# Third unit's state in 64x64 tiles, gate sums of two chunks turned on VectorE, x of two more units through DRAM

## The chip, the core and the metric

The kernel runs on one core of a Trainium2 chip. The engines are TensorE (PE; PEld is its weight load), VectorE (DVE), ScalarE (ACT), GpSimd (POOL) and SyncE (SP), which here issues nearly all DMAs. The metric is the time of one execution in microseconds (us). Three runs of the kernel before took 430.86 to 431.17 us, median 430.98 us.

## What is computed

An mLSTM over 768 time steps for 4 batches of 8 heads of size 40, and a gated two-layer network on its output. In the reference, cut to what matters:

```python
for t in range(S):                                   # B, H, S, D = 4, 8, 768, 40
    m_new  = maximum(f_gate[t] + m, i_gate[t])
    f_stab = exp(f_gate[t] + m - m_new); i_stab = exp(i_gate[t] - m_new); m = m_new
    C = f_stab * C + i_stab * outer(v[t], k[t])      # 40x40 state per head
    n = f_stab * n + i_stab * k[t]
    y[t] = sigmoid(o_gate[t]) * (C @ q[t]) / maximum(abs(n @ q[t]), 1)
x = y as (3072, 320)
h = x @ w_in                                         # 320 -> 2048
out = (h * sigmoid(h)) @ w_out                       # 2048 -> 320
```

## The kernel before

**Units.** Time is cut into 12 chunks of 64. A unit is one chunk of two of the four batches: 24 units, counted from 0; "the third unit" is unit 2. A unit holds 128 rows of tokens (two batches of 64 steps). It makes scores from q and k, weighs them with a decay matrix `D`, adds the contribution of the state `Cm`, normalizes, and gates with o. The result is `x`, 128 tokens by 320 features. It also adds `k` weighted by `kw` times `v` to the state: the matmuls are in `state` (line 692), their sum lies in the tile `pu`, and `carry` (line 735) adds it to `Cm` on VectorE.

**Steps.** Three units make a step of the network: 384 tokens, 8 steps (0 to 7). A step goes through 16 blocks of 128 hidden features, called blocks 0 to 15 here (`fc` in the code). For each, `mm1` multiplies x with w_in into the PSUM tile `ph`, `act` makes tanh on ScalarE (`th`) and the product on VectorE (`g`), and `mm2`, two blocks later, multiplies with w_out into `pout`. So the last two `mm2` of a step come after the first two `mm1` of the next. In step 0 the weights are taken in 32-bit form; from step 1 on every operand is split into a rounded part and a remainder (x into `xh` and `xl`, w_in into `wh` and `wl`), and products of the parts are summed.

**Order.** The order of every engine's instructions is written by hand; no scheduler moves them, and each engine runs its own queue in order. While step j is multiplied, the three units of step j+1 are worked in between, at the blocks that `PLACES` (line 41) gives: in step 0, unit 3 at block 5, unit 4 at block 9, unit 5 at block 12. The table `FILL` (line 1076) adds, for step 0 alone, what is left of the start: making weight parts (`wmake`, which also issues the load of the next part, line 261), the gate sums of later chunks, loads. DMAs issued by SyncE also stand in one queue in order; one that waits holds those behind it.

**x.** mm1 needs x with the features on the partitions. There are two ways. `xpose` (line 784) lets TensorE transpose it by three matmuls against a unit matrix into PSUM, and `xput` (line 796) splits it: xh by ScalarE (line 805), xl by VectorE (line 806). Or, for units in the set `AROUND` (line 930), `turn_out` (line 761) transposes 32x32 blocks on VectorE (line 766) and writes them to DRAM by four DMAs (line 768), `turn_in` (line 772) reads them back two blocks after the unit's place into `px` in SBUF (line 776), and `xput` follows six blocks after the place. Before, units 6 to 23 but unit 8 go around.

**Gate sums.** Running sums of the gates, per batch and head, are made with heads on the partitions (`i_t`) and needed with time on the partitions (`aT`). For chunks 2 and 3 `spread` (line 188) transposes them with TensorE and copies them by VectorE (line 207); for chunks 4 to 11 `spread_far` (line 216) does it with two VectorE transposes (line 228) and four ScalarE copies (line 233).

Of the kernel before, what the change touches and what calls it, by code (L numbers as in the profile page):

```python
# [8 lines left out]
F32 = mybir.dt.float32  # L9
# [5 lines left out]
ALU = mybir.AluOpType  # L15
# [3 lines left out]
B, H, S, D = 4, 8, 768, 40  # L19
L = 64  # L20
NC = S // L
NP = B // 2
NU = NC * NP
# [3 lines left out]
UPS = 3  # L27
# [16 lines left out]
def mlstm_mlp_kernel(  # L44
# [12 lines left out]
    nc = tc.nc  # L57
# [6 lines left out]
    psO = pool("psO", 3, space=PSUM)  # L64
    psH = pool("psH", 2, space=PSUM)
    psP = pool("psP", 1, space=PSUM)
    psU = pool("psU", 1, space=PSUM)
# [9 lines left out]
    ident = cp.tile([128, 128], F32, name="ident")  # L77
# [3 lines left out]
    for k in range(2):  # L81
        m = mask[k * L : (k + 1) * L]
        nc.gpsimd.affine_select(
            out=m, in_=m, compare_op=ALU.is_ge, fill=NEG, base=0,
# [18 lines left out]
    BH = B * H  # L103
    f_t, i_t, m_t, LF, pat = (home[:BH, k * S : (k + 1) * S] for k in range(5))
    aT = cp.tile([128, NC, NP, H], F32, name="aT")

    LFd = dr.tile([NC, BH, L], F32, name="LFd")
# [78 lines left out]
        yield  # L186

    def spread(lo, hi, eng):

        c0, c1 = lo // L, hi // L  # L190
        eng.dma_start(
            LFd[c0:c1].rearrange("c r t -> r c t"),
            LF[:, lo:hi].rearrange("r (c t) -> r c t", t=L),
        )
        yield
        pt = psU.tile([128, 512], F32, tag="u", name=f"pt{lo}")

        for c in range(c0 - 1, c1):
            w = slice(c * L, (c + 2 - (c == NC - 1)) * L)
            nc.tensor.transpose(  # L200
                pt[: w.stop - w.start, c * BH : (c + 1) * BH], i_t[:, w], ident[:BH, :BH]
            )
            if (c - c0) % 3 == 1:
                yield
        for k in range(2):
            r = slice(k * L, (k + 1) * L)
            nc.vector.tensor_copy(  # L207
                aT[r, c0:c1, :, :],
                pt[r, (c0 - k) * BH : (c1 - k) * BH].rearrange(
                    "p (c q d h) -> p c q d h", q=NP, d=2, h=H  # L210
                )[:, :, :, k, :],
            )
        yield


    def spread_far(lo, hi, eng):

        c0, c1 = lo // L, hi // L
        eng.dma_start(
            LFd[c0:c1].rearrange("c r t -> r c t"),  # L220
            LF[:, lo:hi].rearrange("r (c t) -> r c t", t=L),
        )
        yield
        n = (c1 - c0) * BH
        src = i_t[:, lo:hi].rearrange("r (c b x) -> r b c x", b=2, x=32)
        at = home[:BH, : 2 * n].rearrange("x (b c r) -> x b c r", b=2, r=BH)
        for b in range(2):
            nc.vector.transpose(at[:, b], src[:, b])
            yield
        for k in range(2):  # L230
            for b in range(2):
                r = k * L + b * 32
                nc.scalar.copy(
                    aT[r : r + 32, c0:c1].rearrange("p c q h -> p (c q) h"),
                    at[:, b].rearrange("x c (q d h) -> x (c q) d h", q=NP, d=2)[:, :, k, :],
                )
            yield
# [114 lines left out]
    def wload(n):  # L352
        for p in parts[nload[0] : nload[0] + n]:
            p.load()
        nload[0] = min(nload[0] + n, len(parts))

    def wmake(n):

        for p in parts[nmade[0] : nmade[0] + n]:
            p.make()  # L360
            wload(1)
        nmade[0] = min(nmade[0] + n, len(parts))
# [10 lines left out]
    def bank(n, pool_, tag, shape, name):  # L373

        if n < UPS:
            return pool_.tile(shape, F32, tag=tag, name=name)
        return psU.tile(shape, F32, tag="u", name=name)
# [5 lines left out]
    class Unit:  # L383
# [308 lines left out]
        def state(self):  # L692
            n, c, p = self.n, self.c, self.p
            if c == NC - 1:
                return
            if n >= UPS:
                self.pu = [
                    pool_.tile([128, 4, D1], F32, tag=tag, name=f"pu{n}_{tag}")
                    for pool_, tag in ((psU, "u"), (psH, "h"))
                ]  # L700
                for j in range(4):
                    for d in range(2):
                        r = slice(d * L, (d + 1) * L)
                        for a in range(2):
                            nc.tensor.matmul(  # L705
                                self.pu[d][a * 64 : a * 64 + D, j, :],
                                self.kw[r, a * 4 + j, :],
                                self.vt[r, d, a * 4 + j, :],
                                start=True,
                                stop=True,  # L710
                            )
                return
            pu = bank(n, psO, "o", [128, H, D1], f"pu{n}")
            by_d = pu.rearrange("p (d j) f -> p j d f", d=2)
            for j in range(4):
                for a in range(2):
                    nc.tensor.matmul(  # L717
                        by_d[a * 64 : a * 64 + D, j],
                        self.kw[:, a * 4 + j, :],
                        self.vt[:, :, a * 4 + j, :],  # L720
                        start=True,
                        stop=True,
                    )
            self.pu = pu
# [10 lines left out]
        def carry(self, copy=nc.scalar.copy, steps=(0, 1)):  # L735
            n, c, p = self.n, self.c, self.p
            if c == NC - 1:
                return
            pu = self.pu
            for a in range(2):  # L740
                r = slice(a * 64, a * 64 + D)
                v = Cm[p][r, a, :].rearrange("p (h e) -> p h e", e=D1)
                if c == 0:
                    copy(v, pu[r])
                    continue
                if 0 in steps:
                    nc.gpsimd.tensor_tensor(  # L747
                        out=v,
                        in0=v,
                        in1=self.lq[r, :, L - 1].unsqueeze(2).broadcast_to([D, H, D1]),  # L750
                        op=ALU.mult,
                    )
                if 1 not in steps:
                    continue
                for d in range(2) if n >= UPS else ():
                    w = v[:, d * 4 : (d + 1) * 4]
                    nc.vector.tensor_tensor(out=w, in0=w, in1=pu[d][r], op=ALU.add)
                if n < UPS:
                    nc.vector.tensor_tensor(out=v, in0=v, in1=pu[r], op=ALU.add)

        def turn_out(self):

# [164 lines left out]


    units = [Unit(n) for n in range(NU)]
    AROUND = set(range(2 * UPS, NU)) - {3 * UPS - 1}  # L930
    steps = {}

    def block(n):
# [18 lines left out]
    def turn(n):  # L952
# [5 lines left out]
        if n % UPS == 0:  # L958
            steps[n // UPS] = Step(n // UPS)
        if n not in AROUND:  # L960
            units[n].xpose()
            units[n].xput(steps[n // UPS])

    def run(n, it):
        for _ in range(n):
            next(it, None)

    u0, u1, u2, u3, u4 = units[:5]
# [29 lines left out]
    for _ in range(2):  # L998
        nc.tensor.matmul(  # L999
            dummy, ident, ident.unsqueeze(1).broadcast_to([128, 4, 128]), start=True, stop=True  # L1000
        )
    two = gates(2 * L, 4 * L)
    near, far = spread(2 * L, 4 * L, nc.gpsimd), spread_far(4 * L, S, nc.gpsimd)
    late = [gates(4 * L, 8 * L), gates(8 * L, S)]
    widen()
    run(5, gates(0, 2 * L))
# [76 lines left out]
            run(1, near),  # L1083
            u3.reach_act(),
        ),
        1: lambda: (wmake(1), u3.expo_act(), u3.keep(), u3.near(), u4.load_qk()),
        2: lambda: (
            u3.scores(),
            u3.weigh(),
# [45 lines left out]
    for j in range(NSTEP):  # L1135
        st = steps[j]
        for fc in range(NFC):
# [6 lines left out]
            if 0 in at:  # L1144
# [4 lines left out]
                at[0].carry(steps=(0, 1) if j == 0 else (0,))  # L1149
                if at[0].n in AROUND:  # L1150
                    at[0].turn_out()
# [18 lines left out]
            if 1 in at:  # L1170
                turn(at[1].n)
                if j == 0:
                    units[at[1].n + 2].add()
            if 6 in at and at[6].n in AROUND:
                at[6].xput(steps[j + 1])
            if 2 in at and at[2].n in AROUND:
                at[2].turn_in()
# [80 lines left out]
```

## Time and profile before

| what | value |
| --- | --- |
| three runs, median | 430.98 us |
| the profiled execution | 431.02 us |
| its span, first to last instruction | 429.2 us |
| TensorE busy | 422.4 us, 98% |
| VectorE busy | 288.5 us, 67% |
| ScalarE busy | 220.6 us, 51% |
| GpSimd busy | 124.8 us, 29% |

The profile is of one execution, on the only core. A timeline row gives an instruction's start from the span's beginning, its length, engine, line, operation, what it writes and reads, and in brackets the idle time of the engine before it with the instruction that ended it, where that is long enough to be shown. Merged rows (x3) give the length of all together. A 32-bit matmul shows as two records. Matmuls overlap, so what one costs TensorE is the distance to the next one's start.

### The profile page before, as it was taken

The numbers are of one execution on the slowest core, as the hardware profiler recorded it, in microseconds if no ns is written. First come the engines' busy times: TensorE is split into PE (matmuls) and PEld (weight loads), VectorE is DVE, ScalarE is ACT, GpSimd is POOL, SyncE is SP. The second block draws the span as 40 slices with busy tenths as digits, with TensorE's granted clock in tenths as the row PEclk, the third lists the DMA queues.
The fourth block names the chain that finished last, engine by engine and source line by source line (L and its number), as shares of the span: only waits on it lengthen the run. The fifth ranks groups of instructions, "written<-read, shape, count | busy, mean of one in ns | idle before, by whom it ended". The sixth has DMA issues, their size and how long they took to land.

```text
span 429.2 us, 12518 instructions
## 1 busy us (share of the span) xinstructions
PE 422.4 (98%) x5062; PEld 391.7 (91%) x5062; DVE 288.5 (67%) x650; ACT 220.6 (51%) x481; POOL 124.8 (29%) x135
## 2 busy tenths in 40 slices
PE   8999999999999999999999999999999999999995
PEld 4767677899999999999999999999999999999995
DVE  5888799877887677467765677566764756443342
ACT  7684866755755454454454644444454543353331
POOL 5734135234234423043412344034320400000000
PEclk9999999999999999999999999999999999999999
DMA  8999696334551775127660575316750231001001
GB/s 272 387 366 311 177 299 165 117 89 141 159 169 21 196 196 155 31 61 189 174 172 2 123 218 139 118 25 179 209 163 22 54 94 20 18 9 39 2 2 46
DMA packets 62650, 57.17 MB, mean 133 GB/s; under 512 B 31440, under 2 KB 49184, under 8 KB 62592
## 3 DMA queue, kind: packets, MB, share of 16 engines
q1 hardware_dynamic: 62288, 55.94, 45.7%
q8 instruction: 40, 0.66, 0.7%
q10 hardware_dynamic: 208, 0.26, 0.2%
q0 software_dynamic: 96, 0.16, 0.1%
q14 instruction: 18, 0.15, 0.1%
HBM read 48.99 MB, written 7.36 MB: 131 GB/s over the span
## 4 chain that ended last, share of the span: by engine, by line
PE 80%; issue 17%; DVE 1%; ACT 1%; POOL 0%; POOLq 0%; ACTq 0%; DVEq 0%
PE ph L849 35%; PE pout L901 33%; PE p L549 3%; PE p L637 2%; PE p L620 2%; PE dummy L999 1%; PE pu_u L705 1%; PE pu_h L705 1%; DVE D L576 0%; PE e L396 0%; PE px L794 0%; PE pu L717 0%; PE po L604 0%; PE p L794 0%; POOL qt L533 0%
## 5 line engine op out<-in xcount | busy, mean ns | idle before, releaser
L856 ACT ACTIVATE th<-ph 128x384 f32<-128x384 f32 x128 | 62.4, 488 | 106.7 <-PE ph L849 106.2
L849 PE MATMUL ph<-xh,wh 128*128 128x384 f32 x336 | 113.8, 339 | 0.0
L849 PE MATMUL ph<-xl,wh 128*128 128x384 f32 x336 | 113.6, 338 | 0.0
L901 PE MATMUL pout<-woh,gh 128*128 128x320 f32 x336 | 105.5, 314 | 0.0
L901 PE MATMUL pout<-woh,gl 128*128 128x320 f32 x336 | 103.9, 309 | 0.0
L901 PE MATMUL pout<-wol,gh 128*128 128x320 f32 x336 | 103.3, 307 | 0.0
L876 ACT CAST gh<-th 128x384 fp32r<-128x384 f32 x112 | 57.5, 513 | 81.3 <-DVE th L871 69.9
L880 DVE TENSOR_TENSOR gl<-th,gh 128x384 fp32r<-128x384 f32 x112 | 64.6, 577 | 47.5 <-ACT gh L876 47.5
L871 DVE SCALAR_TENSOR_TENSOR th<-th,ph 128x384 f32<-128x384 f32 x112 | 61.4, 548 | 51.1 <-ACT th L856 50.6
L849 PE MATMUL ph<-xh,wl 128*128 128x384 f32 x224 | 75.9, 339 | 0.0
L747 POOL TENSOR_TENSOR Cm<-Cm,lq 40x328 f32<-40x328 f32 x40 | 30.6, 764 | 114.6 <-PE p L637 111.8
L901 PEld LDWEIGHTS pout<-woh,gh 128*128 128x128 f32 x336 | 63.0, 188 | 0.9
L849 PEld LDWEIGHTS ph<-xh,wh 128*128 128x128 f32 x336 | 63.1, 188 | 0.2
L849 PEld LDWEIGHTS ph<-xl,wh 128*128 128x128 f32 x336 | 63.0, 188 | 0.2
L901 PEld LDWEIGHTS pout<-woh,gl 128*128 128x128 f32 x336 | 63.0, 188 | 0.1
L901 PEld LDWEIGHTS pout<-wol,gh 128*128 128x128 f32 x336 | 63.1, 188 | 0.0
L533 POOL TENSOR_TENSOR qt<-qk,lq 104x512 f32<-104x512 f32 x22 | 29.7, 1348 | 99.4 <-ACT lq L529 89.3
L849 PEld LDWEIGHTS ph<-xh,wl 128*128 128x128 f32 x224 | 42.1, 188 | 0.0
L901 PE MATMUL pout<-wo,g 128*128 128x320 f32 x96 | 28.7, 435 | 0.0
L516 POOL TENSOR_TENSOR D<-D,am 128x512 f32<-128x512 f32 x20 | 26.1, 1303 | 4.0 <-DMA D<-LFd 2.5
L508 POOL TENSOR_TENSOR am<-mask,aT 128x512 f32<-128x512 f32 x20 | 24.1, 1205 | 6.6 <-DVE aT L207 5.1
L576 DVE TENSOR_TENSOR D<-p,D 128x512 f32<-128x512 f32 x24 | 16.5, 689 | 13.7 <-PE p L637 12.3
(136 smaller groups left out, 524.4 us busy)
## 6 DMA issues: line engine op xcount, KB each, us to landing
qk<-in_qk_dram SPq DMA_DIRECT2D x24, 512.0 KB, 5.1
ko<-in_ko_dram SPq DMA_DIRECT2D x24, 320.0 KB, 5.3
wro<-in_w_out_dram SPq DMA_DIRECT2D x8, 640.0 KB, 7.3
D<-LFd SPq DMA_DIRECT2D x40, 128.0 KB, 3.1
lq<-LFd SPq DMA_DIRECT2D x40, 128.0 KB, 4.9
wri<-in_w_in_dram SPq DMA_DIRECT2D x8, 512.0 KB, 6.0
vb<-in_vp_dram SPq DMA_DIRECT2D x48, 82.0 KB, 5.1
out_dram<-ob SPq DMA_DIRECT2D x45, 80.0 KB, 2.1
```

Of the source, the lines that this page charges most:

```text
L508: nc.gpsimd.tensor_tensor(out=self.am, in0=mask.unsqueeze(1).broadcast_to([128, H, L]), in1=aT[:, self.c, self.p, :].unsqueeze(2).broadcas ...
L516: nc.gpsimd.tensor_tensor(out=self.Dm, in0=self.Dm, in1=self.am, op=ALU.add)
L533: nc.gpsimd.tensor_tensor(out=self.qt, in0=self.q[:KS], in1=self.lq[:KS], op=ALU.mult)
L549: nc.tensor.matmul(self.ps[d * L : (d + 1) * L, a * 4 + j, :], self.k[r, d * 4 + j, :], self.q[r, d * 4 + j, :], start=True, stop=True,)
L576: nc.vector.tensor_tensor(out=self.Dm, in0=self.ps, in1=self.Dm, op=ALU.mult)
L747: nc.gpsimd.tensor_tensor(out=v, in0=v, in1=self.lq[r, :, L - 1].unsqueeze(2).broadcast_to([D, H, D1]), op=ALU.mult,)
L849: nc.tensor.matmul(ph, w, x, start=(i == 0), stop=(i == len(ops) - 1))
L856: nc.scalar.activation(th, ph, AF.Tanh, scale=0.5)
L871: nc.vector.scalar_tensor_tensor(out=th, in0=th, scalar=1.0, in1=ph, op0=ALU.add, op1=ALU.mult)
L876: nc.scalar.copy(gh, th)
L880: nc.vector.tensor_tensor(out=gl, in0=th, in1=gh.bitcast(F32), op=ALU.subtract)
L901: nc.tensor.matmul(self.po[t], g[:, ts], w, start=(fc == 0 and i == 0), stop=(last and i == len(ops) - 1),)
```

## The change

Three edits, all within step 0 and the start before it.

1. Unit 2's state is multiplied in 64x64 tiles, as the units from 3 on do it: the two halves of the rows apart, into two PSUM tiles (`pu_u` and, for unit 2, `pu_o`), 16 matmuls of 41 columns in place of 8 of 82 columns. `carry` adds the halves with four VectorE instructions in place of two.
2. `spread` becomes what `spread_far` was, for chunks 2 and 3 too: two VectorE transposes and four ScalarE copies in place of three TensorE transposes and two VectorE copies. The VectorE transposes stand in `FILL[1]`, the copies in `FILL[2]`.
3. Units 3 and 4 go around through DRAM like the later ones (unit 5, like unit 8, stays with TensorE). Their `xput` moves from the block after their place to the end of block 11 and of block 15.

```diff
     def spread(lo, hi, eng):
...
-        pt = psU.tile([128, 512], F32, tag="u", name=f"pt{lo}")
-        for c in range(c0 - 1, c1):
...
-            nc.tensor.transpose(
-                pt[: w.stop - w.start, c * BH : (c + 1) * BH], i_t[:, w], ident[:BH, :BH]
-            )
...
-    def spread_far(lo, hi, eng):
...
         for b in range(2):
             nc.vector.transpose(at[:, b], src[:, b])
             yield
...
@@ def state
-            if n >= UPS:
+            if n > 1:
                 self.pu = [
                     pool_.tile([128, 4, D1], F32, tag=tag, name=f"pu{n}_{tag}")
-                    for pool_, tag in ((psU, "u"), (psH, "h"))
+                    for pool_, tag in ((psU, "u"), (psH, "h") if n >= UPS else (psO, "o"))
                 ]
@@ def carry
-                for d in range(2) if n >= UPS else ():
+                for d in range(2) if n > 1 else ():
                     w = v[:, d * 4 : (d + 1) * 4]
                     nc.vector.tensor_tensor(out=w, in0=w, in1=pu[d][r], op=ALU.add)
-                if n < UPS:
-                    nc.vector.tensor_tensor(out=v, in0=v, in1=pu[r], op=ALU.add)
...
-    AROUND = set(range(2 * UPS, NU)) - {3 * UPS - 1}
+    AROUND = set(range(UPS, NU)) - {2 * UPS - 1, 3 * UPS - 1}
...
-    near, far = spread(2 * L, 4 * L, nc.gpsimd), spread_far(4 * L, S, nc.gpsimd)
+    near, far = (spread(lo, hi, nc.gpsimd) for lo, hi in ((2 * L, 4 * L), (4 * L, S)))
...
-        1: lambda: (wmake(1), u3.expo_act(), u3.keep(), u3.near(), u4.load_qk()),
+        1: lambda: (run(2, near), wmake(1), u3.expo_act(), u3.keep(), u3.near(), u4.load_qk()),
```

VectorE at the end of step 0, before. `kw7` is unit 7's key weights, `g0_15` the product of block 15, `wl2` the remainder of the third w_in part; `th1_0` is the first product of step 1.

```order
L863 SCALAR_TENSOR_TENSOR g0_14_1233<-th0_14_1229,ph0_14_1224 128x384
L327 TENSOR_TENSOR wl1_1231<-wi1_514,wh_103 128x512
L228 STREAM_TRANSPOSE home_107<-home_107 32x256
L568 TENSOR_TENSOR kw7_1254<-ko7_1092,D7_1085 128x320
L863 SCALAR_TENSOR_TENSOR g0_15_1265<-th0_15_1261,ph0_15_1256 128x384
L327 TENSOR_TENSOR wl2_1263<-wi2_570,wh_103 128x512
L871 SCALAR_TENSOR_TENSOR th1_0_1284<-th1_0_1284,ph1_0_1275 128x384
```

The same place of VectorE now; `xl1` is the xl tile of step 1, `px4` unit 4's x as read back.

```order
L833 SCALAR_TENSOR_TENSOR g0_14_1252<-th0_14_1248,ph0_14_1243 128x384
L299 TENSOR_TENSOR wl1_1250<-wi1_514,wh_103 128x512
L200 STREAM_TRANSPOSE home_107<-home_107 32x256
L540 TENSOR_TENSOR kw7_1273<-ko7_1111,D7_1104 128x320
L833 SCALAR_TENSOR_TENSOR g0_15_1284<-th0_15_1280,ph0_15_1275 128x384
L299 TENSOR_TENSOR wl2_1282<-wi2_583,wh_103 128x512
L776 TENSOR_TENSOR xl1_845<-px4_1088,xh1_844 128x3x128
L841 SCALAR_TENSOR_TENSOR th1_0_1305<-th1_0_1305,ph1_0_1296 128x384
```

Unit 4's xl has moved from behind block 10 to this place, the last of step 0; the rest stands as it did.

SyncE's DMA queue from the loads of unit 5 (`D5`, `qk5`, `vb2`, `ko5`) on, before; `wro4` is the load of the fifth w_out part, `wrc6` and `wri6` parts of w_in, `lq5` the decay of unit 5.

```order
L464 DMA qk5_706<-in_qk_dram 128x1024
L484 DMA vb2_142<-in_vp_dram 64x328 x2
L475 DMA ko5_710<-in_ko_dram 128x640
L261 DMA wro4_808<-in_w_out_dram 128x2x640
L496 DMA lq5_822<-LFd_115 64x2x256 x2
L261 DMA wrc6_843<-in_w_tail_dram 128x512
L261 DMA wri6_849<-in_w_in_dram 128x2x512
L261 DMA wro5_874<-in_w_out_dram 128x2x640
```

The same place now; `xd1` is the DRAM buffer, `xt3` unit 3's transposed blocks, `px3` its x read back.

```order
L436 DMA qk5_717<-in_qk_dram 128x1024
L456 DMA vb2_142<-in_vp_dram 64x328 x2
L447 DMA ko5_721<-in_ko_dram 128x640
L738 DMA xd1_117<-xt3_812 32x12x32 x4
L233 DMA wro4_825<-in_w_out_dram 128x2x640
L468 DMA lq5_839<-LFd_115 64x2x256 x2
L233 DMA wrc6_855<-in_w_tail_dram 128x512
L233 DMA wri6_861<-in_w_in_dram 128x2x512
L746 DMA px3_882<-xd1_117 128x3x128
L233 DMA wro5_888<-in_w_out_dram 128x2x640
```

The four writes of unit 3's x stand ahead of five loads that stood directly behind `ko5`, and the read stands between two weight loads. Unit 4's five DMAs stand in the same way ahead of the last two w_out parts and of unit 7's loads.

## Rows read from the trace of the kernel before

**Rows 1.** Page, part 1: busy time, share of the span and instructions by engine

```profile
PE 422.4 (98%) x5062; PEld 391.7 (91%) x5062; DVE 288.5 (67%) x650; ACT 220.6 (51%) x481; POOL 124.8 (29%) x135
```

**Rows 2.** Stretches: length; busy PE, PEld, DVE, ACT, POOL; PEclk; DMA share, GB/s

```profile
65.80:80.30 14.50, 14.47 (x138) 10.76 (x131) 14.20 (x30) 9.58 (x21) 7.03 (x7) 1.00 0.63 183
...
78.60:381.70 303.10, 302.83 (x3861) 296.19 (x3860) 206.34 (x466) 148.08 (x329) 86.75 (x82) 1.00 0.42 112
```

**Rows 3.** Timeline of PE: start, length, line, operation; state and transposes

```profile
21.77 0.77 PE L717 MATMUL pu<-vb,kw 128*40 128x82 f32 x16
22.47 1.56 PE L849 MATMUL ph<-x,wi 128*128 128x384 f32 x4
...
28.18 0.37 PE L200 MATMUL pt<-ident,home 32*128 32x32 f32 x3
...
43.67 0.49 PE L794 MATMUL p<-ident,x 128*128 128x128 f32 x3
43.99 1.46 PE L849 MATMUL ph<-x,wi 128*128 128x384 f32 x4
...
66.35 0.21 PE L705 MATMUL pu_u<-vb,kw 64*40 64x41 f32 x2
...
66.67 0.44 PE L637 MATMUL p<-Cm,qt 40*64 40x41 f32 x16
```

**Rows 4.** Line 766 by itself: count, length in ns (min/median/max), first, last start

```profile
L766 DVE STREAM_TRANSPOSE xt<-x x17: 578/578/580, 91.5 to 360.1; 128x384 f32<-128x384 f32 x17
```

**Rows 5.** Timeline of PE where step 1 begins

```profile
78.61 0.58 PE L849 MATMUL ph<-xh,wh 128*128 128x384 f32 x1
79.03 0.34 PE L849 MATMUL ph<-xl,wh 128*128 128x384 f32 x1
```

**Rows 6.** Timeline of DVE in step 0; in brackets idle time before

```profile
42.20 1.05 DVE L757 TENSOR_TENSOR Cm<-Cm,pk 40x164 f32<-40x164 f32 x1
...
53.83 0.81 DVE L282 SCALAR_TENSOR_TENSOR wo<-wro 128x640 uint32<-128x640 uint32 x1
...
65.78 0.81 DVE L282 SCALAR_TENSOR_TENSOR wi<-wri 128x512 uint32<-128x512 uint32 x1 [0.43 <-ACT wri L281]
...
70.68 0.97 DVE L757 TENSOR_TENSOR Cm<-Cm,pk 40x164 f32<-40x164 f32 x1
...
79.65 0.67 DVE L327 TENSOR_TENSOR wl<-wi,wh 128x512 fp32r<-128x512 f32 x1
```

**Rows 7.** Line 806 by itself: the instruction that writes xl

```profile
L806 DVE TENSOR_TENSOR xl<-px,xh x17: 548/1358/1367, 110.6 to 376.6; 128x384 fp32r<-128x384 f32 x17
L806 DVE TENSOR_TENSOR xl<-p,xh x4: 551/554/558, 44.7 to 126.3; 128x384 fp32r<-128x384 f32 x4
```

**Rows 8.** Timeline of POOL around the end of step 0

```profile
64.68 1.36 POOL L533 TENSOR_TENSOR qt<-qk,lq 104x512 f32<-104x512 f32 x1 [5.54 <-ACT lq L529]
...
76.74 2.17 POOL L533 TENSOR_TENSOR qt<-qk,lq 104x512 f32<-104x512 f32 x1 [4.71 <-ACT lq L529]
88.38 1.56 POOL L747 TENSOR_TENSOR Cm<-Cm,lq 40x328 f32<-40x328 f32 x2 [9.47 <-PE p L637]
```

**Rows 9.** Lines 757 and 568 by themselves: Cm adds and kw

```profile
L757 DVE TENSOR_TENSOR Cm<-Cm,pk x38: 312/322/1046, 41.6 to 338.4; 40x164 f32<-40x164 f32 x38
...
L568 DVE TENSOR_TENSOR kw<-ko,D x18: 454/492/1315, 36.8 to 307.3; 128x320 f32<-128x320 f32 x18
```

**Rows 10.** Timeline of the DMA issues on SP

```profile
36.83 0.39 SPq L261 DMA_DIRECT2D wro<-in_w_out_dram  x1
...
92.12 1.88 SPq L768 DMA_DIRECT2D xd<-xt  x4
```

**Rows 11.** Line 261 by itself: from issue to landing of the weight loads

```profile
DMA to landing us min/median/max: 3.3/6.0/8.2
```

**Rows 12.** Timeline of ACT: fifth w_out part, tanh of block 15

```profile
51.17 0.79 ACT L280 ACTIVATE wro<-wro 128x640 f32<-128x640 f32 x1
...
77.44 0.49 ACT L856 ACTIVATE th<-ph 128x384 f32<-128x384 f32 x1 [0.77 <-PE ph L849]
```

More of the change, by code (lines that the diff above doesn't have):

```diff
@@ L188, in spread @@
     def spread(lo, hi, eng):
[L190 to L193, printed above, removed]
-        )
-        yield
-        pt = psU.tile([128, 512], F32, tag="u", name=f"pt{lo}")
-        for c in range(c0 - 1, c1):
-            w = slice(c * L, (c + 2 - (c == NC - 1)) * L)
-            nc.tensor.transpose(
-                pt[: w.stop - w.start, c * BH : (c + 1) * BH], i_t[:, w], ident[:BH, :BH]
[L202 to L213, printed above, removed]
-    def spread_far(lo, hi, eng):
         c0, c1 = lo // L, hi // L
```

## The prediction

> **What bounds the kernel now.** I read the busy shares of the page first. TensorE is busy 98% of the span, no other engine over 67% [rows 1]: what counts is TensorE's own work, and any moment in which it must wait. Then the table by stretches: from 78.6 to 381.7 us TensorE is busy 302.83 of 303.10 us, at the full clock, 2.4 GHz [rows 2]. So a delay that exists at 78.6 us, where step 0 hands over to step 1, is not caught up afterwards, and neither is a gain lost. All parts of the change lie before that point. The same table shows the other engine that matters: VectorE is busy 14.20 of the 14.50 us ahead of 80.3 us [rows 2]. It runs as a queue without a pause there, though not on the average. Last I read the timelines of TensorE, VectorE, ScalarE, GpSimd and of the DMA issues around the places that the change touches.
>
> **What TensorE is spared.** Unit 2's state matmuls start at 21.77 and the next matmul at 22.47 us: 0.70 us. A later unit's state, already in 64x64 tiles, takes from 66.35 to 66.67: 0.32 us. The saving is 0.38. The three transposes of gate sums are 0.37 long; I take 0.30, since the next matmul starts before they end, as in the other rows. The transposes of unit 3's x take 43.67 to 43.99: 0.32; unit 4's are alike, another 0.32 [rows 3]. Together 1.3 us, 1.0 of it before the block of unit 4. If nothing waited, the time would be 431.0 - 1.3 = 429.7 us.
>
> **What the others get.** The four half-width adds of unit 2's state and the turning of gate sums on VectorE and ScalarE come 50 us before the handover. I cost them at zero. They lie beside TensorE's first hidden blocks; if that cover failed they could eat at most what their own edits saved, 0.68 us; and they cannot gain more than that either, since TensorE waits for neither of them before. The new 32x64 transposes are bounded above by the 32-block transpose of 128x384, 0.58 us each [rows 4].
>
> Unit 3 and unit 4 each add one VectorE transpose of 0.58 us [rows 4], four DMAs out and one in on SyncE's queue, and their ScalarE and VectorE splits into xh and xl move: unit 3's from one hidden block after its block to six after (block 11), unit 4's to the very end of block 15. In the queues as built, VectorE's xl of unit 4 stands last in step 0, behind kw, g(15) and the remainder wl of the third weight part. The first matmuls of step 1 read all three units' columns of xh and then of xl, so TensorE cannot run the second of them before that instruction has ended. Behind it TensorE's whole queue stands.
>
> **The wait at the handover.** Before, TensorE begins step 1 at 78.61 with xh and takes xl at 79.03 [rows 5]. VectorE's last wait before that is for ScalarE: 0.43 us, ended at 65.78 by the seventh weight part. From there it is one line of work up to wl, 79.65 + 0.67 = 80.32 [rows 6]; g(15) was not needed by TensorE until three matmul groups later, so this lateness cost nothing. Now xl of unit 4 comes after it. An xl costs 0.55 us when free, 1.36 when it collides [rows 7].
>
> How does the start of the line, 65.78, move? VectorE's block of unit 4 begins 1.0 earlier with TensorE; unit 4's transpose adds 0.58; the moved xl of unit 3 adds 0.55 to 1.36 just ahead of the line; the 0.43 of waiting takes some up. That is -1.0 + 0.58 + 0.55 - 0.43 = -0.3 at best and -1.0 + 0.58 + 1.36 - 0.43 = +0.5 at worst. I take 0.0, the middle, leaning to the collision: qt of unit 5 runs on GpSimd at 64.68 for 1.36 us [rows 8], where this xl will stand. The line itself can shrink: its kw, which stands beside GpSimd's 2.17 us qt [rows 8], is the longest of its kind with 1.315 us where the median is 0.492, and its Cm add at 70.68 took 0.97 where the median is 0.322 [rows 6, 9]. That is 0 to 0.82 and 0 to 0.65; I take 0.05 in all, since the same neighbours stand in the same order, shifted by some tenths, and a collision avoided in one place turns up on the next instruction.
>
> So xl ends at 80.32 + 0.0 + 0.55 - 0.05 = 80.8, and TensorE takes it there instead of at 79.03: +1.8 us. The 1.3 us spared on TensorE are not subtracted: they turn into waiting at this place. The ends are 80.32 - 0.3 + 0.55 - 0.82 - 0.65 = 79.1, +0.1 us, and 80.32 + 0.5 + 0.55 = 81.4, +2.3 us. GpSimd's next instruction after that qt, which ends at 78.91, starts at 88.38 [rows 8], so a contended 1.36 for unit 4's xl is unlikely; it would add 0.81 to the upper end: +3.1.
>
> The profiled execution took 431.02 us, its span 429.2 and 1.8 around it; that is 0.04 above the median of 430.98, which I neglect. **Predicted: 431.0 + 1.8 = 432.8 us.**
>
> **A rule against the change.** The xl that reads a PSUM tile took 551 to 558 ns in all four cases; the one that reads px from SBUF 548 to 1367, median 1358 [rows 7]. The Trainium skill says in SBUF — State Buffer (the part "Reading the diagram") that VectorE and GpSimd share a port pair under an exclusive lock, which a VectorE instruction with two SBUF inputs needs against a GpSimd one that reads SBUF, the loser waiting for the whole instruction. By that rule unit 3's xl waits out qt, 0.81 us that it would not wait in PSUM form; without the rule the sum would be lower by at most that. The trace agrees with it in the spread just quoted.
>
> **Rivals.**
> *Late weights (slower still).* SyncE works in order. The load of the fifth part of w_out was issued at 36.83; now it stands behind unit 3's four DMAs, which wait for the transpose (the Cm adds end at 43.25 [rows 6], now 0.7 earlier with TensorE, then 0.58: 43.1) and take 1.88 to issue [rows 10]: 45.0. Weight loads land after 3.3 to 8.2 us, median 6.0 [rows 11]: 48.3 to 53.2. ScalarE wants them at 51.17 - 1.0 = 50.2 [rows 12]. At the median, 51.0, they are 0.8 late. ScalarE makes two passes of 0.79 at most, so they end by 52.75 [rows 12], and VectorE uses the result only at 53.83 [rows 6]: up to 1.1 of lateness is free. At the slow end, 3.0 late, VectorE's line slips 1.9 and the handover with it: +3.7, 434.7 us. For it speaks the number of small writes in flight; against it that the loads that crowded this one at 36.83 are then gone. Chance 0.14.
>
> *The line relaxes (not slower).* One mechanism: VectorE's collisions with GpSimd. If the shift parts kw from qt and the Cm add from GpSimd's add, 1.47 us go, and xl of unit 4 ends at 79.4: +0.4, 431.4 us. It decides when the line is at least 1.0 us shorter than in the trace. Even without any queue on VectorE, the tanh of block 15 (77.44 and 0.49 long [rows 12]), then g (as large as an xl, 0.55), wl 0.67 and xl 0.55 end at 79.7, or 78.4 with TensorE 1.3 earlier: -0.6 us, 430.4. So a gain beyond 0.9 us has no path that I can see. Chance 0.13 for about the same, 0.03 for faster.
>
> *The wait hits the clock.* TensorE would stand nearly idle for more than 2 us, and the clock could be withdrawn. The granted clock is 1.00 in all stretches [rows 2], but none holds such a gap in the middle, so no row prices it. Three us of matmuls at the lower level, 1.2 GHz, would cost three more: 435.8 us. TensorE: Matmul & The Clock Gate in the Trainium skill (part 1) says that idle stretches return the clock to half rate; nothing in this trace shows it. Chance 0.10.
>
> *Nothing waits.* If the handover did not bind, 429.7 us. Against it stands VectorE's queue order. Its chance is in the 0.03.
>
> **How the numbers follow.** Forecast as reasoned 0.60, late weights 0.14, clock 0.10, about the same 0.13, faster 0.03. A measurement of this kernel tells about 0.2%, 0.86 us, from no change. The forecast's own range, 431.9 to 433.3 (+0.9 to +2.3), is wholly slower, and so are late weights and clock: slower 0.84, same 0.13, faster 0.03. For 8 in 10 the range goes from 431.5, which leaves out about half of the relaxed line and the gain, to 435.3, which leaves out the clock case and the worst landings.
>
> **What would show it.** In the profile after: the state of unit 2 within about 0.35 us and no transposes in blocks 2, 6 and 10; TensorE's first step-1 matmul about 0.5 to 1 us earlier than 78.61, followed by a wait of 2 us or more, ended by VectorE's xl; that xl last in VectorE's step 0, at 80 to 81 us; TensorE without idle time after it. I am wrong if the second matmul of step 1 runs without a wait, if VectorE reaches wl much before 80 us, or if a wait of more than 0.5 us appears earlier, at blocks 9 to 12, ended by a weight load.

## The result: slower, and by more than the range allowed

| | median (lowest to highest), runs |
| --- | --- |
| kernel before, in the same set | 431.4 us (430.86 to 432.80), 6 |
| changed kernel | 436.5 us (434.79 to 437.57), 6 |
| ratio changed / before | 1.0101, 95% interval 1.0073 to 1.0129 |

The change costs 5.1 us in this set, 4.2 us in a second (below). The direction and the place forecast are there; 432.8 us and the upper end of 435.3 us are not.

### The profile page after: what moved, and what is told of

It is laid out like the page before. It is cut to its first block, busy times and chain, and to the rows that moved or that the text cites. A ratio compares the mean times of both kernels' runs of the same rounds, so it can differ in the third digit from the quotient of the medians.

```text
span 434.9 us, 12556 instructions
## 1 busy us (share of the span) xinstructions
PE 424.3 (98%) x5069; PEld 391.4 (90%) x5069; DVE 291.4 (67%) x654; ACT 221.1 (51%) x485; POOL 126.2 (29%) x135
## 4 chain that ended last, share of the span: by engine, by line
PE 63%; issue 17%; DMA 9%; DVE 7%; ACT 1%; SPq 1%; POOL 1%; POOLq 0%; DVEq 0%; ACTq 0%
PE ph L819 28%; PE pout L871 27%; DMA wri<-in_w_in_dram 4%; PE p L521 2%; PE p L609 2%; DMA vb<-in_vp_dram 2%; DMA wro<-in_w_out_dram 2%; PE p L592 2%; DMA D<-LFd 1%; DVE Cm L729 1%; DVE wo L254 1%; PE pu_u L677 1%; DVE g L833 1%; DVE wl L299 0%; PE pu_h L677 0%
## 5 line engine op out<-in xcount | busy, mean ns | idle before, releaser
L871 PE MATMUL pout<-wo,g 128*128 128x320 f32 x96 | 30.5, 455 | 0.0
L480 POOL TENSOR_TENSOR am<-mask,aT 128x512 f32<-128x512 f32 x20 | 25.0, 1251 | 5.6 <-ACT aT L205 4.1
```

Source lines behind the costliest of these rows:

```text
L480: nc.gpsimd.tensor_tensor(out=self.am, in0=mask.unsqueeze(1).broadcast_to([128, H, L]), in1=aT[:, self.c, self.p, :].unsqueeze(2).broadcas ...
L871: nc.tensor.matmul(self.po[t], g[:, ts], w, start=(fc == 0 and i == 0), stop=(last and i == len(ops) - 1),)
```

## The profile after

The changed kernel's part 1 of the page:

```profile
PE 424.3 (98%) x5069; PEld 391.4 (90%) x5069; DVE 291.4 (67%) x654; ACT 221.1 (51%) x485; POOL 126.2 (29%) x135
```

And its table of what TensorE waited for (engine, line, released by: us in total, times, longest):

```profile
PE ph L819 <- DVE xl L776: 1.9, 1, 1.9
PE dummy L969 <- POOL ident masks.py:199: 1.4, 1, 1.4
PE ph L819 <- DVE wi L254: 0.8, 2, 0.4
```

The busy shares hardly differ from [rows 1]. TensorE is busy 1.9 us longer although work was taken from it, a first sign that some of its work ran slower. VectorE carries 2.9 us more. The dummy wait at the start stood in the kernel before as well.

TensorE's timeline at the handover from step 0 to step 1, to be held against [rows 5]:

```profile
78.76 1.77 PE L871 MATMUL pout<-wo,g 128*128 128x320 f32 x6
80.42 0.44 PE L819 MATMUL ph<-xh,wh 128*128 128x384 f32 x1
82.78 0.45 PE L819 MATMUL ph<-xl,wh 128*128 128x384 f32 x1 [1.92 <-DVE xl L776]
...
84.13 3.33 PE L871 MATMUL pout<-wo,g 128*128 128x320 f32 x6
...
88.82 1.78 PE L871 MATMUL pout<-wo,g 128*128 128x320 f32 x6
```

The second matmul of step 1 waits 1.92 us for xl, as forecast. But the first one already comes 1.81 us later than before, not earlier. And behind the wait six pout matmuls take 3.33 us that take 1.77 ahead of it and 1.78 again from 88.82 on. The table of stretches (length; PE busy; PEclk; DMA share, GB/s) says why:

```profile
80.00:82.00 2.00, 0.86 (x3) 1.00 0.82 240
82.00:84.00 2.00, 1.22 (x7) 1.00 0.95 314
84.00:86.00 2.00, 2.00 (x6) 0.55 0.10 37
86.00:88.00 2.00, 2.00 (x7) 0.60 0.00 0
88.00:90.00 2.00, 2.00 (x11) 1.00 0.04 8
```

For some four microseconds after the stand the granted clock is near the lower level, 1.2 GHz. The whole bill of this trace: the matmul that takes xl comes 82.78 - 79.03 = 3.75 us late, the lower clock adds 1.82 (TensorE's third hidden block of step 1 starts 5.57 late), a stand at 164 us adds 0.20, in all 5.77; the span grew by 434.9 - 429.2 = 5.7.

VectorE's timeline, for [rows 6]:

```profile
44.90 0.58 DVE L736 STREAM_TRANSPOSE xt<-x 128x384 f32<-128x384 f32 x1
45.41 0.38 DVE L254 SCALAR_TENSOR_TENSOR wtc<-wrc 128x256 uint32<-128x256 uint32 x1
...
47.95 0.69 DVE L254 SCALAR_TENSOR_TENSOR wi<-wri 128x512 uint32<-128x512 uint32 x1 [0.67 <-ACT wri L253]
...
66.35 1.19 DVE L776 TENSOR_TENSOR xl<-px,xh 128x384 fp32r<-128x384 f32 x1
67.46 0.68 DVE L254 SCALAR_TENSOR_TENSOR wi<-wri 128x512 uint32<-128x512 uint32 x1
...
81.59 0.67 DVE L299 TENSOR_TENSOR wl<-wi,wh 128x512 fp32r<-128x512 f32 x1
82.19 0.54 DVE L776 TENSOR_TENSOR xl<-px,xh 128x384 fp32r<-128x384 f32 x1
```

Unit 4's xl is last and uncontended (0.54 us). Unit 3's, beside GpSimd's qt, took 1.19. VectorE's line from the last w_in part of step 0 (wi at 67.46, 65.78 before) to wl2 starts 1.68 us late and ends 1.94 late. The transpose at 44.90 stands ahead of block 5's weight conversion; it comes up again below.

## The experiments

Ratios are to the kernel before in the same set; its medians there were 431.43 (first four), 431.49 (next four), 431.97 us (e9 to e12). The expectations call two waits by the wrong block. The one for a w_in part "in block 6" is at the first matmul of block 8, which is the first to use that part. The one of 1.0 us "in block 12 for g of block 11" is at the first matmul of block 13, for g of block 12. Below they stand at blocks 8 and 13.

**Unit 4 alone back, then both back (e1, e2).**

```diff
-    AROUND = set(range(UPS, NU)) - {2 * UPS - 1, 3 * UPS - 1}
+    AROUND = set(range(UPS, NU)) - {UPS + 1, 2 * UPS - 1, 3 * UPS - 1}   # e1
+    AROUND = set(range(2 * UPS, NU)) - {3 * UPS - 1}                     # e2
```

> Unit 4's x goes through TensorE again (its transposes in block 10, its xl behind block 10); the rest of the change stays. In the changed kernel's trace the 5.7 us of longer span lie in three places: TensorE is 1.5 us late by the first hidden block, it waits 1.9 us for unit 4's xl at the second matmul of step 1, and its clock is lower for some 6 us behind that wait, which costs 1.8 us. Theory (both the wait and the clock come from unit 4's xl): no wait at step 1, clock 1.00 from 80 to 90 us, 436.7 - 1.9 - 1.8 + 0.3 = 433.3 us if the late start stays, 431.8 if it does not. Rival (VectorE's line is simply too long, whatever stands last in it): a wait of over 1 us at step 1 for another instruction, over 435 us.

> Units 3 and 4 both go through TensorE again: only the first two edits are left (unit 2's state in 64x64 tiles, gate sums on VectorE). If the first two edits are free as forecast (0.68 us less on TensorE, nothing added): 431.4 - 0.7 = 430.7 us, and the first hidden block where it was before. If these two edits are what makes the start 1.5 us late: about 432.2 us, with the weights' first conversion late as in the changed kernel. If unit 3's detour costs nothing, this and the kernel with unit 4 alone turned back differ by 0.3 us.

e1 431.6 us, 1.0001 (0.9985 to 1.0017); e2 431.38 us, 1.0003 (0.9988 to 1.0017). So without unit 4's detour there is no loss. TensorE then does not wait at step 1, as the theory wanted; the rival falls. But neither kernel is faster than before: e2's forecast gain of 0.7 us is not there. Its TensorE comes to block 3 only 0.29 us earlier after its first block than the kernel before (8.21 against 8.50 us), and in block 12 it waits 0.4 us for GpSimd's qt:

```profile
PE p L609 <- POOL qt L505: 0.4, 1, 0.4
```

**The place in VectorE's queue (e3, e6, e7).**

```diff
-            if 6 in at and at[6].n in AROUND:
-                at[6].xput(steps[j + 1])
+            # e3, e7: unit 4's xput five blocks after its place: block 14
+            # e6, e7:
-        (0, 15): ["i2"],
-        (1, 1): ["o1"],
+        (1, 1): ["o1", "i2"],
```

> The full change, but unit 4's split into xh and xl is issued at the end of block 14 instead of block 15, so that on VectorE it stands ahead of the key weights, g(15) and the last remainder wl, which step 1's second matmul does not need. Theory (the place in VectorE's queue makes the wait): the wait of 1.9 us and the lower clock behind it go, 436.7 - 3.7 = 433.0 us with the late start, 431.5 without it. Rival (unit 4's x comes late from DRAM, the place in the queue does not matter): the split now holds VectorE up in block 14 and the time stays at 435 us or more.

> The full change with the remainder wl of the third w_in part made in block 1 of step 1 instead of block 15 of step 0 (it is needed in block 4 of step 1). That takes 0.67 us out of VectorE's line just ahead of unit 4's xl. Theory (VectorE's line sets the handover): the wait falls from 1.9 to about 1.3 us; 435.8 us if the lower clock stays as it is, 434.0 us if a wait of 1.3 us no longer lowers it. Rival (unit 4's xl waits for its data or for ScalarE's xh, not for its place in the line): the wait stays at 1.9 us, 436.5 us.

> Both moves at once: unit 4's split into xh and xl at the end of block 14, and the third remainder wl in step 1. With the first move alone TensorE waited 1.0 us in block 12 for g of block 11 and 0.3 us for unit 4's xl at step 1, and the time was 433.56 us. Theory B (VectorE's line is late from block 11 on, whatever stands last): only the 0.3 us at step 1 can go, 433.3 us. Theory A (the end of step 0 sets it all): nothing waits at step 1, 431.5 us.

e3 433.56 us, 1.0049 (1.0033 to 1.0065); e6 434.69, 1.0080 (1.0056 to 1.0105); e7 434.40, 1.0060 (1.0038 to 1.0082). TensorE's waits, of e6 and then of e3:

```profile
PE p L609 <- issue: 2.1, 1, 2.1
...
PE ph L819 <- DVE xl L776: 1.2, 1, 1.2
```

```profile
69.15 1.56 PE L819 MATMUL ph<-x,wi 128*128 128x384 f32 x4 [1.02 <-DVE g L833]
...
79.35 0.57 PE L819 MATMUL ph<-xh,wh 128*128 128x384 f32 x1
79.93 0.44 PE L819 MATMUL ph<-xl,wh 128*128 128x384 f32 x1
```

Taking 0.67 us out of the line shortens the wait, 1.6 to 1.9 us in the changed kernel, to 1.2 (e6); moving xl ahead all but removes it (e3). So the wait is made by VectorE's queue, as the forecast had it. What stays is TensorE's wait for g: 1.02 us at block 13 in e3, and 0.55 for g of block 11 plus 0.47 for g of block 12 in e7. That is theory B, VectorE is behind from there on. e7 gained nothing on e3.

**Filler for the clock (e4).**

```diff
+            if j == 1 and fc == 0:
+                warm(10, ph)
```

> The full change with ten matmuls of 384 columns added on TensorE ahead of step 1's first matmul (their sum is overwritten). They take about 1.7 us, so TensorE works through most of the 1.9 us in which it stood. Theory (the lower clock comes from the standing): the granted clock stays 1.00 from 80 to 90 us, the xl that is waited for ends as late as before, and the time is 436.5 - 1.8 = 434.7 us. Rival (the lower clock has another cause than the wait): the clock falls to about 0.74 in 85 to 90 us again and the time stays at 436.5 us or above.

434.63 us, 1.0076 (1.0052 to 1.0099). TensorE's handover, and then the table of stretches behind it:

```profile
80.31 1.79 PE L953 MATMUL ph<-maskb,identb 128*128 128x384 bf16 x10
81.80 0.47 PE L821 MATMUL ph<-xh,wh 128*128 128x384 f32 x1
82.36 0.45 PE L821 MATMUL ph<-xl,wh 128*128 128x384 f32 x1
```

```profile
84.00:86.00 2.00, 2.00 (x10) 1.00 0.46 154
86.00:88.00 2.00, 2.00 (x11) 1.00 0.00 0
```

xl is taken as late as ever (+3.33 against the trace of before), yet the clock stays at 2.4 GHz and the span is 3.2 us longer, no more. One such trace could be chance, for the clock does not fall in every execution of the changed kernel (below). But the mean granted clock, which is on record for every run, says the same: it is 0.998 or 0.999 in all six runs of e4, and 0.994 to 0.996 in seven of the fourteen of the changed kernel, as in the two traces where the fall is seen. So the theory holds: the lower clock comes from TensorE standing there.

**Unit 4 alone around (e5).**

```diff
+    AROUND = set(range(UPS, NU)) - {UPS, 2 * UPS - 1, 3 * UPS - 1}
```

> Unit 3's x goes through TensorE again (its VectorE transpose of 0.58 us goes, its xl stands behind block 6 instead of block 11); unit 4 goes around through DRAM with its xl last in step 0, as in the changed kernel. Theory A (only the place of unit 4's xl counts): the wait of 1.9 us and the lower clock stay, 0.3 us more for TensorE's transposes, 436 to 437 us. Theory B (VectorE's whole line from block 9 on is too long, and unit 3's xl of 1.2 us in block 11 and its transpose are part of it): the line ends up to 1.8 us earlier, the wait shrinks to well under 1 us, the clock stays at 1.00, 436.5 - 1.8 - 1.8 + 0.3 = 433.2 us.

433.75 us, 1.0057 (1.0036 to 1.0077), near theory B in time. Against the changed kernel it saves 2 to 3 us: unit 3's detour costs nothing alone (e1) but adds to the loss where unit 4 goes around too. The handover still costs TensorE 1.3 us, in two pieces; the waits of its trace:

```profile
PE p L609 <- POOL qt L505: 1.0, 1, 1.0
...
PE ph L819 <- DVE xl L776: 0.7, 1, 0.7
PE ph L819 <- ACT xh L775: 0.6, 1, 0.6
```

**The same kernels again (e8, e13, e14: changed; e15, e16: before).** No edit.

> The changed kernel once more, unaltered, for a second trace of it. Theory (the 1.5 us by which TensorE was late at the first hidden block are chance: how fast the first loads land differs from one execution to the next, whatever the kernel): the first hidden block starts somewhere else, between 0.5 us earlier and 1.5 us later than in the trace of before, while the wait at step 1 and the lower clock are there again; 436.5 us. Rival (the change makes the start late): 1.2 to 1.8 us late again.

> The changed kernel a third time, for another trace. In three traces with the wait at step 1 (1.92 and 1.66 us in the changed kernel, 1.59 us with filler matmuls in the start) the clock fell behind it twice and cost 1.8 us each time. Theory A (a wait of 1.6 us or more lowers the clock nearly always): low clock again, 435.5 to 437 us. Theory B (it falls in some executions only, which spreads this kernel's times over 434.1 to 437.6 us): clock 1.00 and about 434.2 us is as likely. The matmul in step 3 stands for 0.2 us or more by either.

> The changed kernel a fourth time, as the one before: theory A low clock and 435.5 to 437 us, theory B as likely clock 1.00 and about 434.2 us.

> The kernel before a second time, for another trace. Theory (the first hidden block starts early or late from one execution to the next, with how fast the first loads come, whatever the kernel; the trace that was read, at 19.99 us, is one draw): it starts anywhere between 19.4 and 21.5 us, TensorE never waits more than 0.5 us from 22 to 381 us, and there is no stand in step 3. Rival (the kernel before starts always near 20.0 us, and the changed one's late start is its own): 19.9 to 20.1 us.

> The kernel before a third time, as the one before it: by the theory a start of the first hidden block between 19.4 and 21.5 us, by the rival 19.9 to 20.1 us.

e8 435.65 us, 1.0092 (1.0071 to 1.0113). e13 435.34, e14 436.46, e15 431.83, e16 433.57 us are single times. The start of the first hidden block, the matmul that takes xl, and what comes behind it until the span's end, from TensorE's timelines:

| trace | first block | xl taken at | wait | rest of the span | clock behind it |
| --- | --- | --- | --- | --- | --- |
| before | 19.99 | 79.03 | none | 350.2 | full |
| e15 | 20.08 | 79.85 | none | 350.2 | full |
| e16 | 20.32 | 81.51 | none | 350.3 | full |
| changed | 21.46 | 82.78 | 1.92 | 352.1 | lower |
| e8 | 19.69 | 81.16 | 1.66 | 352.9 | lower |
| e13 | 19.55 | 82.61 | 1.60 | 351.0 | full |
| e14 | 20.40 | 83.13 | 1.66 | 351.6 | full |

Three of the rows, of e8, e13 and e14:

```profile
81.16 0.45 PE L819 MATMUL ph<-xl,wh 128*128 128x384 f32 x1 [1.66 <-DVE xl L776]
```

```profile
82.61 0.44 PE L819 MATMUL ph<-xl,wh 128*128 128x384 f32 x1 [1.60 <-DVE xl L776]
```

```profile
83.13 0.45 PE L819 MATMUL ph<-xl,wh 128*128 128x384 f32 x1 [1.66 <-DVE xl L776]
```

The late start is chance: the changed kernel's other traces begin at 19.55 to 20.40, those of before at 19.99 to 20.32. Theory B holds for the clock: it fell in two of four traces. Its time, 434.2 us, does not: e13 and e14 took 435.34 and 436.46 us at the full clock, so the clock is only a part of what separates fast executions from slow ones. And the trace that the forecast read was the earliest of three at the handover; e15 and e16 reach it 0.8 and 2.5 us later. In e16 TensorE waits 1.07 us at 39.93, more than the 0.5 us that e15's theory allowed.

**The stand in step 3 (e9).**

```diff
-    small(32)
+    small(40)
```

> The full change with eight more of the 64-column filler matmuls that already stand in the start (40 in place of 32; about 0.2 us, where TensorE waits anyway). All later instructions of TensorE keep their order but stand 16 further on in its program. In five traces of kernels with the full change's TensorE program up to there, TensorE stood 0.2 to 2.1 us at one and the same matmul in step 3 (near 160 to 164 us), with no semaphore to wait for; in traces of kernels with more or fewer instructions ahead of it, not. Theory (the stand depends on where that matmul falls in TensorE's program, as with code that is loaded in pieces): no stand at that matmul, perhaps one elsewhere; 0.3 to 0.5 us faster than the changed kernel, 435.5 us. Rival (it is bound to what the matmul works on): it stands there again, 436 us.

434.86 us, 1.0075 (1.0050 to 1.0100); TensorE does not stand at that matmul. In all eight traces of kernels with the changed TensorE program up to there it does, 0.2 to 2.1 us, and without a releaser; e8's row, and e6's with the two stretches around it:

```profile
163.93 0.19 PE L609 MATMUL p<-Cm,qt 40*64 40x41 f32 x1 [1.03 <-issue]
```

```profile
163.94 0.19 PE L609 MATMUL p<-Cm,qt 40*64 40x41 f32 x1 [2.10 <-issue]
```

```profile
160.00:168.00 8.00, 5.90 (x145) 0.84 0.42 106
168.00:175.00 7.00, 7.00 (x43) 0.94 0.56 150
```

In the kernels with other counts of TensorE instructions ahead of it (before, e1, e2, e4, e5, e10, e11) there is none. So it hangs on where the matmul falls in TensorE's program, not on its data; for the move itself e9 is one trace. A second such stand, 0.4 to 0.7 us at one matmul near 250 to 255 us, comes and goes: it is there in e1, e3, e7, e10, e11, e12 and e14, not in the others. What TensorE waits for at either place no run shows.

**Relief for VectorE (e10, e11, e12).**

```diff
-                if at[0].n in AROUND:
+                if at[0].n in AROUND and j > 0:
                     at[0].turn_out()
...
             if j == 0:
                 FILL[fc]()
+                if 0 in at and at[0].n in AROUND:
+                    at[0].turn_out()
```

e10 and e11 stand on e1; e11 also has unit 3's `xput` in block 10. e12 has unit 4 around too, both splits a block earlier, and `i1`, `i2` moved to blocks 0 and 1 of step 1.

> Unit 4 through TensorE as in the kernel that measured 431.6 us, and unit 3's transpose with its four DMAs moved from ahead of block 5's weight conversion to behind it (also on SyncE's queue, where the load of the fifth w_out part now stands ahead of them). In all six traces with unit 3 around, TensorE waits 0.3 to 0.9 us in block 6 for a w_in part; in the three without, never. Theory (the 0.58 us transpose on VectorE delays the weight chain VectorE, ScalarE, VectorE behind it): this wait goes, 431.6 - 0.5 = 431.1 us. Rival (the weights are late because their loads are): the wait in block 6 stays, since this load was issued long before, and the time stays at 431.6 us.

> As the kernel before it in this set, and unit 3's split into xh and xl moved from block 11 to block 10, away from the GpSimd multiplication qt of 1.3 us beside which its xl took 1.2 us in place of 0.55. Theory: the xl takes 0.55 us, the wait of 0.3 us for g in block 12 goes, TensorE keeps the 0.7 to 1.0 us that it was spared: 430.6 us, 0.8 below the kernel before. Rival (GpSimd's qt is what block 12 waits for next): a wait of 0.3 us or more there for qt, 431.1 us.

> The full change with every move that relieves VectorE: the transposes and their DMAs of units 3 and 4 behind their blocks' weight conversion, their splits in blocks 10 and 14, the second and third remainder wl in blocks 0 and 1 of step 1. Theory (VectorE's line in step 0 is all that eats what TensorE is spared): 431.4 - 1.3 = 430.1 us, no wait at step 1. Rival (from block 11 on, other waits, GpSimd's qt and the two extra transposes of 0.58 us, still make VectorE late): 431.5 to 432.5 us.

e10 432.59 us, 1.0014 (0.9996 to 1.0032): a miss; the wait in block 8 is still 0.34 us, and block 13 waits 1.02 for g. e11 431.85, 1.0006 (0.9983 to 1.0028): xl takes 0.58 us away from qt, blocks 8 and 13 no longer wait for VectorE, but block 12 now waits for qt, as the rival said. e12 433.60, 1.0049 (1.0024 to 1.0075): no wait at step 1, yet 1.0 us for g of block 11 in block 12, also the rival's, and slower than the rival's 431.5 to 432.5. e11's row of VectorE's timeline and its wait:

```profile
61.26 0.58 DVE L776 TENSOR_TENSOR xl<-px,xh 128x384 fp32r<-128x384 f32 x1
```

```profile
PE p L609 <- POOL qt L505: 0.4, 1, 0.4
```

No version beats the kernel before beyond its interval.

## Why the prediction was wrong, step by step

*TensorE's own saving: there, but smaller.* Unit 2's state went from 0.70 to 0.45 us here, 23.27 to 23.72 (forecast 0.32), and the transposes are gone. But a part was lost at once. In block 2 `pout` takes 1.94 us to the next matmul, where it took 1.71; of before, and then of now with the last add of `carry`:

```profile
25.85 1.78 PE L901 MATMUL pout<-wo,g 128*128 128x320 f32 x6
27.56 0.69 PE L549 MATMUL p<-qk 40*64 40x64 f32 x32
```

```profile
23.27 0.23 PE L677 MATMUL pu_u<-vb,kw 64*40 64x41 f32 x2
...
23.72 1.56 PE L819 MATMUL ph<-x,wi 128*128 128x384 f32 x4
...
27.11 2.02 PE L871 MATMUL pout<-wo,g 128*128 128x320 f32 x6
29.05 0.69 PE L521 MATMUL p<-qk 40*64 40x64 f32 x32
...
27.88 0.33 DVE L729 TENSOR_TENSOR Cm<-Cm,pu_o 40x164 f32<-40x164 f32 x1
```

Unit 2's second tile `pu_o` comes from the same pool of three PSUM tiles as the three tiles of `pout`, and the last of these goes on right after that add ends at 28.2. This is in every trace of the changed kernel. No run took the tile from elsewhere, so the reason is read from the order, not tested. It comes with the first edit, whose four adds the forecast put at zero: of the 0.68 us that the first two edits were to spare, about 0.3 us are left at block 3.

TensorE was to arrive 0.5 to 1 us earlier than 78.61 at step 1 and came at 80.42, 79.06, 80.57 and 81.03 in the four traces, against 78.61, 79.44 and 81.09 before: 80.3 and 79.7 on average.

*"VectorE's block of unit 4 begins 1.0 earlier with TensorE": a step that failed ahead of the handover.* Counted from the first hidden block, TensorE reaches unit 4's block 9 on average 0.4 us earlier (30.9 against 31.3 us). The forecast counted the two new VectorE transposes only as length on VectorE's last line. Unit 3's also stands ahead of a weight chain, VectorE's wtc at 45.41, ScalarE, then wi at 47.95, and TensorE takes that wi in block 8. It waits 0.3 to 0.9 us there in 12 of 13 traces with unit 3 around and in none of 5 without. But the transpose is not the main cause. In the kernel before, that wi ends at 47.37 and block 8 starts at 47.42:

```profile
46.68 0.69 DVE L282 SCALAR_TENSOR_TENSOR wi<-wri 128x512 uint32<-128x512 uint32 x1 [0.51 <-ACT wri L281]
47.42 1.56 PE L849 MATMUL ph<-x,wi 128*128 128x384 f32 x4
```

The same 0.05 us or so lies between the two in all 18 traces. So TensorE was held by this weight part already, without a listed wait. The 0.32 us of unit 3's transposes could hardly be kept there, and e10, which moves the VectorE transpose out of the way, still waits 0.34 (e11, with the same move, does not: its part came 0.4 us sooner after block 6). Unit 4's transpose does the like to block 9's chain: with ScalarE late, GpSimd's qt comes late, and in e5 TensorE waits 1.0 us for it, where e2, without either detour, waits 0.4. What falls beside that qt on VectorE takes longer. In the changed kernel's first trace and in e8 it is unit 3's xl, and block 13 hardly waits. In e3, e13 and e14 it is an instruction of the gate sums, 1.3 us in place of 0.28, and the scan behind it takes 1.22 in place of 0.67; there g of block 12 is late and block 13 waits 1.02 us. Both in e13:

```profile
64.93 1.31 DVE L176 TENSOR_SCALAR home<-home 32x256 f32<-32x256 f32 x1
...
67.70 1.22 DVE L180 TENSOR_TENSOR_SCAN home<-home 32x256 f32<-32x256 f32 x1
```

*The wait at the handover: right in mechanism and place, one term mis-sized.* Over four traces against three, the matmul that takes xl comes at 82.4 against 80.1 us: +2.3, where the forecast had +1.8 and +2.3 as its upper end. The traces of one kernel lie 2 to 2.5 us apart here, so the mean is rough. VectorE's wl2 ends 0.5 us later on average (80.64 to 82.61, against 80.32 to 82.73). The line up to it starts where it did (67.0 us in both), as forecast, but by luck: of its terms the 1.0 was 0.4, and 0.0 was called the middle of -0.3 and +0.5, which is 0.1. What failed is the line's length. The forecast took 0.05 us off; it grew by 0.5 (14.9 against 14.4 us). xl adds the half microsecond behind it, as forecast. By the trace that was read alone the changed kernel's profiled run would be +3.75: it began 1.47 us later, by chance.

*"The wait hits the clock": the step that failed behind the handover.* Its time, 435.8 us, was the forecast's wait and 3 us on top, but at a chance of 0.10 it stood outside the sum and the range. It came in two traces of four, 1.8 us each, 0.9 on average. The Trainium skill, TensorE: Matmul & The Clock Gate (part 1), says that idle stretches return the clock to half rate; the trace agrees, at 0.55 and 0.60 behind the 1.92 us wait, and e4 bears it out by taking the idle time away. Not every stand did it: 1.60 and 1.66 us (e13, e14) left it at 1.00.

*"TensorE without idle time after it": wrong.* The stand in step 3 costs 0.2 to 1.0 us in the four traces, and e14 stands another 0.4 us near 255 us; 0.7 on average. Nothing in the forecast allowed for it.

The sum of means: 2.3 + 0.9 + 0.7 = 3.9 us where the forecast had 1.8, against 4.2 and 5.1 us between the medians of the two sets.

*The base.* The forecast added to 431.0 us and neglected 0.04. In the later sets the kernel before had a median of 431.4 to 432.0 us over 11 to 29 runs: the three runs shown, and the profiled one, were fast draws. That is 0.4 us or more.

*Late weights*: in e8 (at 51.49 us) and e1 ScalarE waits 0.5 us for that load, in e9 0.8, less than the 1.1 us that the forecast held free; in the other traces of the changed kernel not at all. *The line relaxes*: kw7 did shrink to 0.44 us and the Cm add to 0.31, as that rival hoped, but the time came back at once on the instructions now beside GpSimd's (home 1.50, xl 1.19), as the forecast argued. There the port rule of SBUF — State Buffer in the Trainium skill ("Reading the diagram") fits: unit 3's xl takes 1.19 us beside qt and 0.58 where e11 puts it.

## What to carry to other kernels

Work taken from the bound engine is worth what the next engine has free at that place: here VectorE was nearly full from block 9 on (busy 9.94 of 10.80 us from 55.0 to 65.8, then 14.20 of 14.50), so the sum had to be made on its queue from each moved instruction to all that depends on what stands behind it, through ScalarE and GpSimd too. A place where the bound engine starts right on another engine's result, as at block 8, ends a saving made ahead of it, even where no wait is listed. When a forecast puts a wait on TensorE, what the wait does to its clock is a further term with a chance, not an alternative. One trace is one draw; a second trace of the same kernel shows which of its gaps are its own.

## What the runs showed of the hardware

The kernel before reaches the same matmul of step 1 at 79.03, 79.85 and 81.51 us in three executions. Standing idle lowers the clock by chance at about the same length: 1.66 us did in e8 and did not in e14. It does so away from the handover too: behind e6's 2.10 us stand at 163.94 the clock is 0.84 and 0.94 in the two stretches. A mean clock of 0.996 or less stands on record in 1 of 67 runs of the kernel before (sets of e1 to e12) and in 4 of 12 of e12, whose one trace shows no wait at step 1; where the clock fell in those runs no trace shows. A matmul that waits for nothing the profile shows can stand up to 2.1 us, and in one trace eight small matmuls 150 us ahead of it made that go.
